# Tracing order kept on one engine instead of five, in a fused attention, Fourier mixing and feed-forward kernel

## The chip, the core and the metric

The kernel runs on one NeuronCore of a Trainium2 chip. The core has five instruction queues, each worked through strictly in the order in which its instructions stand: TensorE (PE, matrix products), VectorE (DVE), ScalarE (ACT), GpSimd (POOL) and SyncE (SP, which here only issues transfers). ACT and POOL can issue transfers too. The metric is the device time of one execution in microseconds (us); lower is better.

## The reference, cut to what matters

```python
# attention, per batch (8) and head (8): seq 576, head size 64
scores = q @ k.T / 8 ; cum = cumsum(max(s, 0))
scores = where(causal, -1e9, scores + minimum(-(cum_i - cum_j), 0))
attn = softmax(scores); x = attn @ v                 # -> (8, 576, 512)
# mixing and feed-forward
mixed = real(fft(fft(x, axis=seq), axis=model))
u = x + mixed
un = (u - mean(u)) / sqrt(var(u) + 1e-6)
out = u + relu(un @ w_ch1) @ w_ch2                   # 512 -> 2048 -> 512
```

## The kernel before

Everything is computed in pairs of numbers (a rounded high part and the rest, `h` and `l` in names), so most products are two or three matmuls.

**Attention.** 32 steps `i`, each one pair of heads of one batch. `load(i)` fetches q and k (`qk`); `high` casts them on ACT into the tile `KQ`; `low` makes the low parts, `k1` on DVE (L572) and `q1` on POOL (L575), out of copies that SP moves across partitions. `maxes(i)` computes each row's maximum: PE writes scores to PSUM (`pm`, L596), DVE reduces them (`Mx`, L603), PE transposes the ten columns (`pmt`) and SP writes them back into `KQ` (L613). `scores(i)` multiplies again (`ps`, L639 and L640), ACT takes the exponential (`P`, L643), POOL zeroes the upper triangle (L620, L624). `av(i)` multiplies by v (`pavA`, `pavB`, L672); ACT copies the result to `stage`. `post(i)` inverts the row sums: they travel by DMA into `sums` (L683), DVE adds and inverts (L693, L694), SP sends them through DRAM (`rd` L697, `rb` L701), POOL multiplies (L709), and SP spreads the result into `xs`.

**Mixing.** `folds` and `fourier`, once per batch, do the two transforms as matmuls with tables (`dcos`, `scos`, ...), which `load_tables` fetches through POOL's queue at step 2 of the main loop.

**Feed-forward.** `mlp()` goes over 9 token tiles of 512 and 16 slices of the hidden width. Layer 1 is 12 matmuls into `h` (L284), ACT and DVE split the result into `zh` (L289) and `zl` (L314), layer 2 is 12 matmuls into four `acc` banks (L340 to L342). Beside it run `mean`, `centre`, `deviation` and `output` of the neighbouring tiles, which load `uj` tiles over SP (L142), subtract the mean on DVE (L194) and write the result (`o`, L227 to L232).

**The weights' conversion.** The weights arrive as 64-bit floating point (`wP`). `convert(f, x, wc, buf)` turns one piece into a high and a low 32-bit part: a transfer in (L80), one DVE step (L84), one ACT step (L86), three DVE steps (L88, L89, L91), three POOL steps (L94, L96, L98) and a transfer out to `wD` in DRAM (L100). There are 20 pieces of 512 columns, in three buffers (two named `wide`, one `cv`), during main-loop steps 0 to 7, and 24 pieces of 256 columns, in two halves of `cv`, during steps 8 to 13. The feed-forward part starts once the first ten slices are converted, and fetches weights from `wD` through ACT's queue (`w`, L131).

**What sets the order.** All these are Python generators that yield a cost, and `weave` interleaves them: it always advances the stream that is behind by its share. The result is the order in which instructions are traced. The main loop runs under `tc.manual_schedule(engines={...})`: on the engines named there, instructions are issued in the order traced. On an engine that is not named, the framework's scheduler decides the order at build time: it walks through a modelled time and gives a free engine an instruction that is then ready by its model, the earliest traced first. In the kernel before, all five engines are named.

Of the kernel before, what the change touches and what calls it, by code (L numbers as in the profile page):

```python
# [8 lines left out]
F32 = mybir.dt.float32  # L9
F32R = mybir.dt.float32r  # L10
AF = mybir.ActivationFunctionType
ALU = mybir.AluOpType
BF16 = mybir.dt.bfloat16
I32 = mybir.dt.int32
# [26 lines left out]
def fused_kernel(ctx, tc, qkT, vA, sP, wP, tabD, tabS, corr, out):  # L41
    nc = tc.nc
# [11 lines left out]
    wD = dram.tile([NF, 128, 2, 2, 512], F32, name="wD")  # L54
# [8 lines left out]
    wbias = const.tile([128, 1], F32, name="wbias")  # L63
    nc.vector.memset(wbias, -8.0 * WEXP)

    def pool(name, **kw):
        return tc.tile_pool(name=name, bufs=1, reuse_waits="tile", **kw)


    mlp0 = ctx.enter_context(tc.tile_pool(name="mlp0", bufs=1))  # L70

# [4 lines left out]
    def convert(f, x, wc, buf):  # L76

        k, o = divmod(x * wc, 512)
        words, e = buf[:, 0:2 * wc], buf[:, 2 * wc:3 * wc]
        nc.sync.dma_start(out=words, in_=wP[f, :, wc * x:wc * x + wc].bitcast(I32))  # L80
        hi = words.rearrange("p (n w) -> p n w", w=2)[:, :, 1]
        lo = words.bitcast(U16).rearrange("p (n w) -> p n w", w=4)[:, :, 1]
        yield 2.0
        nc.vector.tensor_scalar(e, hi, 0x7FF00000, None, op0=ALU.bitwise_and)  # L84
        yield 1.0
        nc.scalar.activation(e, e, AF.Relu, bias=wbias, scale=8.0)  # L86
        yield 1.0
        nc.vector.scalar_tensor_tensor(out=e, in0=hi, scalar=-0x80000000, in1=e, op0=ALU.bitwise_and, op1=ALU.bitwise_or)  # L88
        nc.vector.tensor_scalar(hi, hi, 0xFFFFF, 0x100000, op0=ALU.bitwise_and, op1=ALU.bitwise_or)  # L89
        yield 0.5  # L90
        nc.vector.scalar_tensor_tensor(out=hi.bitcast(F32), in0=lo, scalar=2.0 ** -16, in1=hi, op0=ALU.mult, op1=ALU.add)  # L91
        yield 1.0
        v = e.bitcast(F32)
        nc.gpsimd.tensor_mul(v, hi.bitcast(F32), v)  # L94
        wh, wl = words[:, 0:wc], words[:, wc:2 * wc]
        nc.gpsimd.tensor_copy(wh.bitcast(F32R), v)  # L96
        yield 0.5
        nc.gpsimd.tensor_sub(wl.bitcast(F32R), v, wh.bitcast(F32))  # L98
        yield 1.5
        nc.sync.dma_start(out=wD[f, :, k, :, o:o + wc], in_=words.bitcast(F32).rearrange("p (s n) -> p s n", s=2))  # L100
        left[f] -= wc
        yield 1.5

    CONVERT = 9.0
    left = [1024] * NF
# [1 line left out]
    def convert_w(pieces, wc, places):  # L107

        def way(n):
            yield n * CONVERT / len(places)  # L110
            for f, x in pieces[n::len(places)]:
                yield from convert(f, x, wc, places[n]())
        yield from mixed(*[[way(n), 1.0] for n in range(len(places))])
# [617 lines left out]
    stages = mlp()  # L731

    order = ctx.enter_context(ExitStack())
    ET = mybir.EngineType
    order.enter_context(tc.manual_schedule(engines={ET.PE, ET.Activation, ET.DVE, ET.Pool, ET.SP}))
    for i in range(NP + 5):
        streams = []
        if 2 <= i <= NP + 1:
# [201 lines left out]
```

## Time and profile before

| what | value |
|---|---|
| median of 3 runs | 1648.24 us (1647.5 to 1652.3) |
| the profiled execution | 1643.94 us, of it 1642.2 us from the first instruction to the last |
| PE busy | 1386.4 us, 84% of the span |
| DVE, ACT, POOL busy | 700.8, 526.9, 491.6 us (43%, 32%, 30%) |
| mean granted TensorE clock | 0.921 |

The page of the profile gives busy time per engine, the span in 40 slices, DMA queues, the chain of work that ended last and groups of instructions. Other views used below: busy time in chosen stretches, the waits (who waited for whom), one tile's instructions, and the timeline. In a row of waits, "PE pm L596 <- DVE Mx L603: 26.1, 17, 4.7" means that PE's instruction at line 596 that writes `pm` stood idle 26.1 us in total, 17 times, 4.7 us at most, until DVE's line 603 was done. SPq is SP's queue issuing transfers.

### The profile page before, as it was taken

The numbers are of one execution on the slowest core, as the hardware profiler recorded it, in microseconds if no ns is written. First come the engines' busy times: TensorE is split into PE (matmuls) and PEld (weight loads), VectorE is DVE, ScalarE is ACT, GpSimd is POOL, SyncE is SP. The second block draws the span as 40 slices with busy tenths as digits, with TensorE's granted clock in tenths as the row PEclk, the third lists the DMA queues.
The fourth block names the chain that finished last, engine by engine and source line by source line (L and its number), as shares of the span: only waits on it lengthen the run. The fifth ranks groups of instructions, "written<-read, shape, count | busy, mean of one in ns | idle before, by whom it ended". The sixth has DMA issues, their size and how long they took to land.

```text
span 1642.2 us, 18338 instructions
## 1 busy us (share of the span) xinstructions
PE 1386.4 (84%) x6244; PEld 1116.2 (68%) x6244; DVE 700.8 (43%) x1567; ACT 526.9 (32%) x1149; POOL 491.6 (30%) x522
## 2 busy tenths in 40 slices
PE   4666665778877899889999889979897999999998
PEld 3444453556765687678777667757785887888887
DVE  5766745454445433543454334334423332222322
ACT  3443433433333423343344333334322221111210
POOL 4766654343433231233223212232212121020200
PEclk9877796889988999989999899989998999999999
DMA  5776554656655556645755564464456445320100
GB/s 160 198 209 199 168 175 156 183 173 183 213 170 179 164 183 171 210 123 184 223 174 171 178 188 153 140 205 145 142 164 218 164 157 166 129 77 26 54 25 26
DMA packets 118137, 259.84 MB, mean 158 GB/s; under 512 B 16047, under 2 KB 44112, under 8 KB 118043
## 3 DMA queue, kind: packets, MB, share of 16 engines
q1 hardware_dynamic: 87115, 150.25, 30.1%
q10 hardware_dynamic: 29232, 105.92, 20.4%
q0 software_dynamic: 1696, 2.50, 0.8%
q8 instruction: 50, 0.82, 0.2%
q14 instruction: 44, 0.36, 0.1%
HBM read 197.96 MB, written 36.70 MB: 143 GB/s over the span
## 4 chain that ended last, share of the span: by engine, by line
PE 52%; DMA 22%; DVE 8%; POOL 6%; issue 5%; ACT 3%; SPq 3%; ACTq 0%; POOLq 0%; DVEq 0%
PE h L284 19%; PE acc L340 6%; PE acc L342 6%; PE acc L341 6%; DMA uj<-uD 5%; PE pavB L672 5%; DMA w<-wD 3%; DMA cv<-in_wP_dram 3%; DMA wD<-cv 2%; PE pm L596 2%; PE ps L639 2%; PE ps L640 1%; DVE trash L603 1%; DMA uD<-xs 1%; DMA wD<-wide 1%
## 5 line engine op out<-in xcount | busy, mean ns | idle before, releaser
L314 DVE SCALAR_TENSOR_TENSOR zl<-h,zh 128x512 fp32r<-128x512 f32 x144 | 99.0, 688 | 354.9 <-ACT zh L289 354.4
L643 ACT ACTIVATE P<-ps 128x320 f32<-128x320 f32 (+4 forms) x384 | 146.6, 391 | 235.0 <-PE ps L640 230.8
L284 PE MATMUL h<-uch,w 128*128 128x512 f32 x688 | 189.7, 418 | 20.2 <-ACT uch L196 18.1
L596 PE MATMUL pm<-KQ 128*128 128x256 f32 (+3 forms) x384 | 144.0, 391 | 73.5 <-DVE Mx L603 35.5
L639 PE MATMUL ps<-KQ 128*128 128x256 f32 (+2 forms) x384 | 132.1, 346 | 78.0 <-DVE Mx L603 30.4
L603 DVE CUSTOM_DVE_ANT_0 trash<-pm,amask 128x128 bf16<-128x128 f32 (+3 forms) x256 | 123.8, 483 | 163.5 <-PE pm L596 157.5
L672 PE MATMUL pavB<-P,va 128*128 128x320 f32 (+2 forms) x640 | 170.4, 419 | 9.7 <-DVE Mx L603 7.2
L284 PEld LDWEIGHTS h<-uch,w 128*128 128x128 f32 x688 | 135.6, 202 | 54.2 <-ACT uch L196 24.2
L289 ACT ACTIVATE zh<-h 128x512 fp32r<-128x512 f32 x144 | 85.8, 596 | 261.0 <-PE h L284 260.5
L672 PEld LDWEIGHTS pavB<-P,va 128*128 128x128 f32 x640 | 129.9, 213 | 55.4 <-issue 15.2
L340 PE MATMUL acc<-zh,w 128*128 128x512 f32 x332 | 139.8, 421 | 27.9 <-DVE o L227 23.1
L596 PEld LDWEIGHTS pm<-KQ 128*128 128x128 f32 x384 | 79.1, 210 | 105.8 <-DVE Mx L603 48.9
L639 PEld LDWEIGHTS ps<-KQ 128*128 128x128 f32 x384 | 78.7, 205 | 101.0 <-DVE Mx L603 34.3
L620 POOL TENSOR_SCALAR_AFFINE_SELECT P<-P 128x512 f32<-128x512 f32 x64 | 49.9, 779 | 313.4 <-ACT P L643 312.9
L341 PE MATMUL acc<-zh,w 128*128 128x512 f32 x332 | 135.7, 409 | 0.0
L342 PE MATMUL acc<-zl,w 128*128 128x512 f32 x332 | 135.5, 408 | 0.0
L640 PE MATMUL ps<-q,k 128*128 128x256 f32 (+2 forms) x384 | 123.2, 323 | 0.0
L284 PE MATMUL h<-uch,W 128*128 128x512 f32 x464 | 117.4, 395 | 6.3 <-ACT uch L196 6.3
L284 PEld LDWEIGHTS h<-uch,W 128*128 128x128 f32 x464 | 88.0, 190 | 26.3 <-ACT uch L196 8.0
L204 POOL TENSOR_TENSOR t<-t,uj 128x512 f32<-128x512 f32 x27 | 36.1, 1339 | 225.3 <-ACT uj L202 224.3
L340 PE MATMUL acc<-zh,W 128*128 128x512 f32 x244 | 96.4, 395 | 8.3 <-DVE o L227 7.4
L575 POOL TENSOR_TENSOR q<-qk,q 64x576 fp32r<-64x576 f32 x64 | 94.5, 1478 | 20.4 <-DMA q<-KQ 15.5
(148 smaller groups left out, 2398.0 us busy)
## 6 DMA issues: line engine op xcount, KB each, us to landing
w<-wD ACTq DMA_DIRECT2D x169, 512.0 KB
uj<-uD SPq DMA_DIRECT2D x104, 256.0 KB
qk<-in_qkT_dram SPq DMA_DIRECT2D x32, 576.0 KB
W<-wD ACTq DMA_DIRECT2D x32, 512.0 KB
va<-in_vA_dram SPq DMA_DIRECT2D x32, 480.0 KB
q<-KQ SPq DMA_DIRECT2D x32, 288.0 KB
k<-KQ SPq DMA_DIRECT2D x32, 288.0 KB
rb<-rd SPq DMA_DIRECT2D x64, 144.0 KB
```

What stands on the lines that cost most here:

```text
L284: nc.tensor.matmul(h[:, :n], w[:, a, j * 128:(j + 1) * 128], b[:, j, :n], start=i == 0, stop=i == 11)
L314: nc.vector.scalar_tensor_tensor(out=zl[:, :n], in0=h[:, :n], scalar=0.0, in1=zh[:, :n].bitcast(F32), op0=ALU.max, op1=ALU.subtract)
L340: nc.tensor.matmul(acc[:, :n], b[:, 0, cs], y[:, :n], start=g == 0, stop=False)
L341: nc.tensor.matmul(acc[:, :n], b[:, 1, cs], y[:, :n], start=False, stop=False)
L342: nc.tensor.matmul(acc[:, :n], b[:, 0, cs], z[:, :n], start=False, stop=g == NF - 1)
L575: nc.gpsimd.tensor_sub(q1[64:128, h], qk[0:64, h], q1[0:64, h].bitcast(F32))
L596: nc.tensor.matmul(p[:, :n], qy[:, h, 128 * c:128 * c + 128], ky[:, h, k0:k0 + n], start=True, stop=True)
L603: nc.vector.tensor_tensor_reduce(out=trash[:nq, :n], in0=p[:nq, :n], in1=amask[:nq, m0:m0 + n], scale=1.0, scalar=first if x else NEG, op0 ...
L639: nc.tensor.matmul(p[:, :n], ky[:, h, ksl], qy[:, h, a:a + n], start=True, stop=False)
L640: nc.tensor.matmul(p[:, :n], k1[:, h, ksl], q1[:, h, a:a + n], start=False, stop=True)
L643: nc.scalar.activation(P[:, o:o + a + n - lo], p[:, lo - a:n], AF.Exp, scale=0.125)
L672: nc.tensor.matmul(p[:, a - lo:n], va[:, c, vs], P[:, o:o + w], start=c == 0, stop=c == cs[-1])
```

## The change

Three edits. `manual_schedule` names TensorE alone, so that DVE, ACT, POOL and SP get their order from the scheduler. Each step of the conversion is traced under `behind(engine)`, which lets the scheduler place it only behind the instruction that was traced last on that engine; nothing else has such a tie. The conversion's two transfers per piece are issued by POOL instead of SP, and the costs it yields between steps are spread a little differently (their sum stays 9.0).

```diff
+    ET = mybir.EngineType
+    def behind(engine):
+        return tc.issue_after(next(i for i in reversed(nc.cur_bb.bb.instructions) if i.engine == engine))
...
-        nc.sync.dma_start(out=words, in_=wP[f, :, wc * x:wc * x + wc].bitcast(I32))
+        with behind(ET.Pool):
+            nc.gpsimd.dma_start(out=words, in_=wP[f, :, wc * x:wc * x + wc].bitcast(I32))
...
-        yield 2.0
-        nc.vector.tensor_scalar(e, hi, 0x7FF00000, None, op0=ALU.bitwise_and)
+        yield 2.5
+        with behind(ET.DVE):
+            nc.vector.tensor_scalar(e, hi, 0x7FF00000, None, op0=ALU.bitwise_and)
...
-        nc.gpsimd.tensor_mul(v, hi.bitcast(F32), v)
+        with behind(ET.Pool):
+            nc.gpsimd.tensor_mul(v, hi.bitcast(F32), v)
...
-        yield 1.5
-        nc.sync.dma_start(out=wD[f, :, k, :, o:o + wc], in_=words.bitcast(F32).rearrange("p (s n) -> p s n", s=2))
+        yield 0.5
+        with behind(ET.Pool):
+            nc.gpsimd.dma_start(out=wD[f, :, k, :, o:o + wc], in_=words.bitcast(F32).rearrange("p (s n) -> p s n", s=2))
         left[f] -= wc
-        yield 1.5
+        yield 2.0
...
-    order.enter_context(tc.manual_schedule(engines={ET.PE, ET.Activation, ET.DVE, ET.Pool, ET.SP}))
+    order.enter_context(tc.manual_schedule(engines={ET.PE}))
```

Line numbers in the kernel after are 13 higher behind the conversion (L603 becomes L616, L693 L706, L575 L588); the conversion's own lines become L87 (in), L92, L95, L98, L99, L102, L106, L108, L110 and L113 (out). PE's instructions stand in the same order in both kernels. On the other four, what stands where has changed throughout. Counted over the two orders, DVE's inversions of the sums stand on average 15 places earlier among its 1569 instructions, its subtractions of the mean (L194, now L207) 28 places earlier, the maxima 7 places later and the conversion's steps 5 to 7 places later; ACT's casts into `KQ` stand 16 to 19 places earlier.

POOL, near the start of the program, before:

```order
L575 TENSOR_TENSOR q_159<-qk,q_159 64x576 x2
L575 TENSOR_TENSOR q_219<-qk,q_219 64x576 x2
L620 AFFINE_SELECT P<-P 128x4x128
L624 AFFINE_SELECT P<-P 128x64
L94 TENSOR_TENSOR wide<-wide 128x512
L96 CAST wide<-wide 128x512
L98 TENSOR_TENSOR wide<-wide 128x512
```

and now, from the last two of the nine table transfers on:

```order
L375 DMA ssin_89<-in_tabS_dram 96x870
L376 DMA cor<-in_corr_dram 97x258
L588 TENSOR_TENSOR q_219<-qk,q_219 64x576 x2
L87 DMA wide<-in_wP_dram 128x1024
L633 AFFINE_SELECT P<-P 128x4x128
L87 DMA wide<-in_wP_dram 128x1024
L637 AFFINE_SELECT P<-P 128x64
L633 AFFINE_SELECT P<-P 128x4x128
L637 AFFINE_SELECT P<-P 128x64
L106 TENSOR_TENSOR wide<-wide 128x512
```

The conversion's loads now stand between the zeroings of the triangle, and the nine table transfers (`dcos` to `cor`), which stood 22 rows further on, stand ahead of the second step's `q1`.

SP, in steps 2 and 3 of the main loop, before (L80 and L100 are the conversion's transfers):

```order
L697 DMA rd<-sums 32x36
L683 DMA sums<-stage 16x1x36
L80 DMA wide<-in_wP_dram 128x1024
L701 DMA rb<-rd 64x576 x2
L100 DMA wD<-cv 128x1024
L613 DMA KQ_118<-mt 1x10x128
L578 DMA va<-in_vA_dram 128x5x192
L683 DMA sums<-rows 16x1x36
L80 DMA cv<-in_wP_dram 128x1024
L538 DMA qk<-in_qkT_dram 128x1152
L567 DMA q_729<-KQ_119 64x2x576
```

and now:

```order
L710 DMA rd<-sums 32x36
L551 DMA qk<-in_qkT_dram 128x1152
L696 DMA sums<-stage 16x1x36
L714 DMA rb<-rd 64x576 x2
L591 DMA va<-in_vA_dram 128x5x192
L696 DMA sums<-rows 16x1x36
L580 DMA q_728<-KQ_119 64x2x576
L626 DMA KQ_118<-mt 1x10x128
```

The conversion's transfers are gone from this queue; the fetch of q and k (`qk`), which waits for POOL and DVE to have read the buffer's old content, now stands ahead of `rb`, and the maxima's way back into `KQ` stands behind the sums and the copy of the next step's `q1`.

DVE, about the middle of the program, before (step of `k_4761`):

```order
L572 TENSOR_TENSOR k_4761<-qk,KQ_118 64x576
L599 TENSOR_REDUCE M_4756<-pm 64x1
L603 ISA trash,Mx_127<-pm,amask,M_4756 64x320
L603 ISA Mx_127 64x1
L603 ISA trash,Mx_127<-pm,amask 128x128
L603 ISA Mx_127 128x1
L693 TENSOR_SCALAR sums<-sums 32x36
L694 RECIPROCAL sums<-sums 32x36
L603 ISA trash,Mx_127<-pm,amask 128x256
L603 ISA Mx_127 128x1
```

and the same step now:

```order
L184 TENSOR_TENSOR t<-t,uj 128x512
L185 TENSOR_TENSOR t<-t,uj 128x512
L706 TENSOR_SCALAR sums<-sums 32x36
L163 TENSOR_TENSOR tl<-t,th 128x512
L707 RECIPROCAL sums<-sums 32x36
L327 SCALAR_TENSOR_TENSOR zl<-h,zh 128x512
L207 TENSOR_TENSOR uj<-uj,mu 128x512
L585 TENSOR_TENSOR k_4761<-qk,KQ_118 64x576 x2
L207 TENSOR_TENSOR uj<-uj,mu 128x512
L616 ISA trash,Mx_127<-pm,amask 128x128
L616 ISA Mx_127 128x1
```

The inversion of the sums, the sums for the mean and the mean's subtractions stand ahead of all of this step's maxima, where the inversion stood in the midst of them before.

More of the change, by code (lines that the diff above doesn't have):

```diff
@@ L79, in convert @@
         words, e = buf[:, 0:2 * wc], buf[:, 2 * wc:3 * wc]
-        nc.sync.dma_start(out=words, in_=wP[f, :, wc * x:wc * x + wc].bitcast(I32))
+        with behind(ET.Pool):
+            nc.gpsimd.dma_start(out=words, in_=wP[f, :, wc * x:wc * x + wc].bitcast(I32))
         hi = words.rearrange("p (n w) -> p n w", w=2)[:, :, 1]
         lo = words.bitcast(U16).rearrange("p (n w) -> p n w", w=4)[:, :, 1]
-        yield 2.0
-        nc.vector.tensor_scalar(e, hi, 0x7FF00000, None, op0=ALU.bitwise_and)
+        yield 2.5
+        with behind(ET.DVE):
+            nc.vector.tensor_scalar(e, hi, 0x7FF00000, None, op0=ALU.bitwise_and)
         yield 1.0
-        nc.scalar.activation(e, e, AF.Relu, bias=wbias, scale=8.0)
+        with behind(ET.Activation):
+            nc.scalar.activation(e, e, AF.Relu, bias=wbias, scale=8.0)
         yield 1.0
-        nc.vector.scalar_tensor_tensor(out=e, in0=hi, scalar=-0x80000000, in1=e, op0=ALU.bitwise_and, op1=ALU.bitwise_or)
-        nc.vector.tensor_scalar(hi, hi, 0xFFFFF, 0x100000, op0=ALU.bitwise_and, op1=ALU.bitwise_or)
+        with behind(ET.DVE):
+            nc.vector.scalar_tensor_tensor(out=e, in0=hi, scalar=-0x80000000, in1=e, op0=ALU.bitwise_and, op1=ALU.bitwise_or)
+            nc.vector.tensor_scalar(hi, hi, 0xFFFFF, 0x100000, op0=ALU.bitwise_and, op1=ALU.bitwise_or)
         yield 0.5
-        nc.vector.scalar_tensor_tensor(out=hi.bitcast(F32), in0=lo, scalar=2.0 ** -16, in1=hi, op0=ALU.mult, op1=ALU.add)
+        with behind(ET.DVE):
+            nc.vector.scalar_tensor_tensor(out=hi.bitcast(F32), in0=lo, scalar=2.0 ** -16, in1=hi, op0=ALU.mult, op1=ALU.add)
         yield 1.0
         v = e.bitcast(F32)
-        nc.gpsimd.tensor_mul(v, hi.bitcast(F32), v)
+        with behind(ET.Pool):
+            nc.gpsimd.tensor_mul(v, hi.bitcast(F32), v)
         wh, wl = words[:, 0:wc], words[:, wc:2 * wc]
@@ L733, in fused_kernel @@
     order = ctx.enter_context(ExitStack())
-    ET = mybir.EngineType
-    order.enter_context(tc.manual_schedule(engines={ET.PE, ET.Activation, ET.DVE, ET.Pool, ET.SP}))
+    order.enter_context(tc.manual_schedule(engines={ET.PE}))
     for i in range(NP + 5):
```

## The prediction

> **What bounds the kernel now.** I read the busy time by stretches first, then who waits for whom in the stretches that have slack, then the rows of the steps that move.
>
> By stretches (PE busy, PEld, DVE, ACT, POOL with their counts, then granted clock, DMA share, GB/s):
>
> ```profile
> 60.00:320.00 260.00, 166.04 (x674) 126.65 (x674) 152.41 (x346) 106.18 (x241) 145.17 (x150) 0.79 0.62 182
> 320.00:520.00 200.00, 161.91 (x727) 128.74 (x725) 98.17 (x248) 70.20 (x163) 74.92 (x95) 0.89 0.62 190
> 520.00:760.00 240.00, 213.76 (x1019) 174.20 (x1019) 103.88 (x243) 89.69 (x199) 68.17 (x71) 0.94 0.55 169
> 760.00:1200.00 440.00, 393.10 (x1851) 319.70 (x1852) 179.71 (x435) 157.85 (x359) 115.71 (x119) 0.95 0.56 172
> 1200.00:1642.00 442.00, 419.62 (x1879) 344.41 (x1877) 126.33 (x198) 80.04 (x145) 55.20 (x49) 0.98 0.33 110
> ```
>
> From 1200 us on PE is busy 95% at a clock of 0.98: nothing to win there, little to lose. From 60 to 320 us PE is idle 94 of 260 us, and no other engine is full either (DVE 59%, POOL 56%): that stretch is bound by waits between queues. From 520 to 1200 us PE still idles 73 of 680 us. So order decides in the first 520 us, and somewhat up to 1200.
>
> Who makes PE wait, 60 to 320 us:
>
> ```profile
> PE pm L596 <- DVE Mx L603: 26.1, 17, 4.7
> PE ps L639 <- DVE Mx L603: 17.3, 2, 13.2
> PE pavB L672 <- DVE Mx L603: 7.0, 6, 2.7
> PE pavA L672 <- DVE Mx L603: 2.0, 2, 1.6
> ```
>
> That is 52.4 us of waiting for DVE's maxima, more than half of PE's idle time there. What holds DVE in the same stretch:
>
> ```profile
> DVE cv L84 <- DMA cv<-in_wP_dram: 28.6, 7, 6.4
> DVE wide L88 <- ACT wide L86: 20.4, 10, 4.7
> DVE cv L88 <- ACT cv L86: 15.4, 5, 5.4
> DVE wide L84 <- DMA wide<-in_wP_dram: 5.2, 5, 1.8
> ```
>
> All four are the conversion: 69.6 us in which DVE stands at a conversion step that is not ready, with maxima behind it. 52.4 against 69.6 gives the exchange rate that I use below: 0.75 us of PE for each us that the conversion holds a queue in this stage. It is an estimate, and an upper one, since some of the maxima were late for other reasons.
>
> **The change part by part.**
>
> *POOL issues 88 transfers more* (44 in, 44 out). Its only transfers so far are the nine tables:
>
> ```profile
> L359 POOL DMA_DIRECT2D dcos<-in_tabD_dram x2: 744/847/950, 66.9 to 69.7; - x2
> L361 POOL DMA_DIRECT2D scos<-in_tabS_dram x2: 571/574/576, 68.6 to 71.2; - x2
> 76.66 0.55 POOL L363 DMA_DIRECT2D cor<-in_corr_dram  x1 [4.35 <-DMA dcos<-in_tabD_dram]
> ```
>
> The 40 transfers of the large pieces and the 24 loads of small ones have one run of memory per partition, like scos and cor: 64 x 0.57 = 36.5 us. The 24 small stores have two, like dcos: 24 x 0.85 = 20.4 us. Together 57 us, in the stretch from 60 to 520 us, where POOL is busy 145.17 + 74.92 = 220 of 460 us. It rises to 277 us, 60%. I cost the issuing itself at nothing: POOL's idle 240 us cover it. Without that cover it would cost PE up to 57 x 0.75 = 43 us.
>
> *The loads' waits move from SP's queue to POOL's.* A piece may be loaded only when the store before it in its buffer has landed. SP waits for that now (all of the span):
>
> ```profile
> SPq L80 <- DMA wD<-cv: 53.5, 20, 7.2
> SPq L80 <- DMA wD<-wide: 50.0, 8, 8.8
> ```
>
> 103.5 us in 28 waits, 3.7 us each. On POOL the triangle's zeroings (PE's `pavA` and `pavB` need them), the `q1` subtractions (`ps` needs them) and the conversion's own steps queue behind such a wait, and a load that goes out later makes DVE's L84 (now L92) wait longer, with maxima behind. POOL is busy 48% of the time there, so 48% of the waiting falls on work: 50 us, and at 0.75 that is **+37 us**. From below: 0, if the scheduler puts each load where its store has landed. From above: all of it, 103.5 x 0.75 = 78.
>
> *SP is rid of 88 transfers and of those waits.* What PE suffers from SP's queue is short in the profile:
>
> ```profile
> PE ps L639 <- DMA KQ<-mt: 8.9, 4, 2.2
> ```
>
> I take half, **-4 us** (bounds -9 and 0; the maxima's way back now stands behind the sums, which eats part of it). The page "DMA: Bandwidth & Descriptors" of the Trainium skill, section "Issuing engines are not separate DMA queues", speaks against even that: transfers from any engine run on the same 16 DMA engines, and another issuer saves only the time to issue. By it this term is 0 and the sum 4 us higher; the 8.9 us row is too small to judge it.
>
> *DVE's conversion steps stand 5 to 7 places later, behind maxima that are ready.* This attacks the 52.4 us. All of it would be -52; nothing would be 0, if the loads come later by as much as the steps. I take half, **-26 us**.
>
> *Steps that hang on transfers run ahead.* The inversion of the sums stands 15 places earlier on DVE, ahead of maxima. It waits for a transfer out of the previous product. Pieces of the chain that ended last, with start and length:
>
> ```profile
> 111.36 2.42 DMA sums<-stage
> 165.49 3.82 DMA sums<-stage
> ```
>
> So 3.1 us each, and 32 such places. Now it hardly costs anything, because it stands late:
>
> ```profile
>   DVE sums L693: 5.0, 1
> ...
> SPq L697 <- DVE sums L694: 126.9, 16, 24.5
> ```
>
> DVE waited for sums once; SP, which sends the result on, waited for DVE 7.9 us a time. 15 places are 15 x 1642/1569 = 16 us of DVE's queue at its mean pace, twice the 7.9 us that were spare, so I expect DVE to meet an unlanded transfer there once per step. The ten steps before 520 us, at 0.75: 10 x 3.1 x 0.75 = 23. The 22 later ones in a stretch where DVE is 42% busy and PE has banks in reserve, at a third of that rate: 22 x 3.1 x 0.25 = 17. Together **+40 us**; bounds 0 and 32 x 3.1 x 0.75 = 74.
>
> *The subtractions of the mean stand 28 places earlier.* That should remove PE's wait for their result,
>
> ```profile
> PE h L284 <- ACT uch L196: 24.4, 11, 6.5
> ```
>
> of which I take three quarters, **-18 us** (bounds -24 and, since they too stand behind loads and ahead of maxima, +24). The longer wait for `o` stays, since those steps keep their places:
>
> ```profile
> PE acc L340 <- DVE o L227: 30.5, 15, 5.8
> ```
>
> *The tables go out at about 19 us instead of 67.* POOL's first table transfer, and the `q1` work between which they now stand:
>
> ```profile
> 66.93 0.95 POOL L359 DMA_DIRECT2D dcos<-in_tabD_dram  x1
> 15.85 2.77 POOL L575 TENSOR_TENSOR q<-qk,q 64x576 fp32r<-64x576 f32 x2 [5.04 <-DMA q<-KQ]
> 29.12 2.77 POOL L575 TENSOR_TENSOR q<-qk,q 64x576 fp32r<-64x576 f32 x2 [10.50 <-DMA q<-KQ]
> ```
>
> With `cor` above they take POOL from 66.93 to 77.21 us, 10.3 us, of it 4.35 us in which the ninth waits for the first to land. 18.6 + 10.3 = 28.9 us; the next `q1` starts at 29.1 now, so it just fits. The 2.5 MB also share the DMA engines with the first q, k and v. Bounds: -10 (the time at 67 us comes free) to +10; I take 0.
>
> The profiled execution took 1643.94 us, 1.7 us of it around this span:
>
> ```profile
> span 1642.2 us, 18338 instructions
> ```
>
> Sum: 0 + 37 - 4 - 26 + 40 - 18 + 0 = **+29 us**. Against the profiled execution that is 1673. The median of the runs is 1648.24, 4.3 us above that execution, so the forecast for the median is 1648 + 29 = **1677 us**, slower by 1.8%.
>
> **The rivals.**
>
> *Faster: the queues stop blocking each other.* In the traced order an engine stands at an instruction that is not ready while ready ones wait behind it; the scheduler picks ready ones. If its modelled time is close to the real one, the +37 and +40 vanish and the gains are whole: -52 - 24 - 9 = -85, or, at the values taken, -48: 1600 us, and with a third of the two losses left 1626. For it: the 69.6 us above are exactly such blocking, and no engine but PE is over 60% busy. Against it: the order is fixed at build, and real transfers vary (2.4 and 3.8 us in the two `sums` rows, waits of 3.7 us on average and up to 8.8 for `wD`), so a place that suits one landing is wrong for the next. It decides if DVE's waits at L92 and L706 stay below about 80 us in all. Middle of this case: 1612 us.
>
> *The same.* The losses come out at 60% (46 us) and meet the gains of 48. For it: POOL's and DVE's idle halves. Against it: it needs two sums of independent size to agree to 5 us. 1648 us.
>
> *Much slower: POOL becomes the bound of the first 520 us.* 220 us of work, 57 of issuing and 103.5 of waiting are 380 of 460 us with no overlap; each `q1` and each zeroing then comes late, and the conversion, which the feed-forward part waits for, stretches. Price: 78 for the waits in place of 37, 43 for the issuing in place of 0: 1677 + 41 + 43 = 1761 at the end, 1720 halfway. For it: POOL's own nine transfers already show 4.35 us lost to one landing. Against it: 80% is still not full.
>
> The conversion's first DVE step (shortest, median, longest in ns):
>
> ```profile
> L84 DVE TENSOR_SCALAR cv<-cv x30: 279/300/1483, 45.0 to 460.5; 128x256 int32<-128x256 int32 x24, 128x512 int32<-128x512 int32 x6
> ```
>
> The page "SBUF — State Buffer" of the Trainium skill, section "SBUF: two separate sides", would add to the much slower case: it says that GpSimd cannot write its transfers' descriptors while VectorE runs an instruction in a two-port mode. If each of the 88 waited once for a conversion step of 0.30 us, the median of L84, POOL would lose 26 us more, an estimate from that page and that row, and the sum would rise by 26 x 0.48 x 0.75 = 9 us; no row before shows such a wait.
>
> **How the numbers follow.** My forecast, slower by some 10 to 60 us, has 0.50; much slower 0.14; the same 0.10; faster 0.26. A difference of 0.3% (5 us) is about what a measurement of this kernel can tell from none. So faster 0.26, same 0.10, slower 0.64. The forecast's own range is 1655 to 1710. The range that holds 8 in 10 must take in half of the faster case and half of the much slower one, which leaves 0.13 and 0.07 out: 1612 to 1735.
>
> **What would show it.** The conversion's last store goes out at 464.7 us now:
>
> ```profile
> L100 SPq DMA_DIRECT2D wD<-cv x30: 320/379/1100, 57.2 to 464.7; - x30
> ```
>
> Right: POOL waiting for `wD` at L87 for 80 us or more; DVE waiting at L92 from 60 to 320 us longer than the 33.8 us (28.6 + 5.2) that it waits for loads at L84, and at L706 for `sums` some tens of us; PE's idle time from 60 to 520 us, 94 + 38 = 132 us, grown by 20 or more, with a lower granted clock there; the last store later than 464.7 us; `uch` gone from PE's waits; the stretch that begins at 1200 us now unchanged in length. Wrong: PE's waits for `Mx` halved in the first 320 us and the last store out no later than now, or a loss that sits behind 1200 us, where no term of mine lies.

## The result and the profile after

The kernel after takes 1562.23 us (median of 3 runs, 1559.16 to 1562.93) against 1648.24 us: a ratio of 0.947 (0.944 to 0.950). It is 86 us faster, where 29 us slower was forecast; the time lies below the range of 1612 to 1735 us. The profiled execution after has a span of 1560.2 us, that of before 1642.2 us. Disturbed runs are left out of the times and ratios below (of the four runs with the `uj` loads tied, two were). A profile shows one execution, and that one can lie several us off the median: 1643.9 against 1648 to 1652 us before, 1535.9 against 1528.8 us for the kernel with all four engines free. So a difference of a few us between parts of two profiles says little.

Since TensorE's order is the same in both kernels, the k-th matmul of one is the k-th of the other, and the span can be cut at the same points of the program. First before, then after, cut where before passes 60, 320, 522 and 1200 us (start:end and length in us, then busy us and instructions of PE, PEld, DVE, ACT, POOL, then granted clock, DMA share, GB/s):

```profile
60.00:320.00 260.00, 166.04 (x674) 126.65 (x674) 152.41 (x346) 106.18 (x241) 145.17 (x150) 0.79 0.62 182
320.00:522.00 202.00, 161.91 (x727) 128.74 (x725) 100.17 (x250) 70.33 (x163) 76.84 (x97) 0.89 0.62 191
522.00:1200.00 678.00, 606.87 (x2870) 493.90 (x2871) 281.58 (x675) 247.40 (x555) 181.96 (x187) 0.94 0.55 170
1200.00:1637.00 437.00, 419.62 (x1879) 344.41 (x1877) 124.16 (x195) 80.04 (x145) 55.20 (x49) 0.98 0.33 109
```

```profile
61.00:311.00 250.00, 162.03 (x674) 130.81 (x673) 169.92 (x353) 108.00 (x244) 174.22 (x196) 0.77 0.60 187
311.00:508.00 197.00, 157.53 (x727) 128.60 (x726) 103.12 (x257) 72.10 (x165) 101.04 (x131) 0.90 0.63 189
508.00:1122.00 614.00, 578.02 (x2872) 480.43 (x2871) 264.33 (x669) 247.15 (x551) 180.50 (x185) 0.98 0.64 190
1122.00:1555.00 433.00, 416.84 (x1879) 344.34 (x1878) 126.81 (x189) 79.59 (x144) 55.69 (x49) 0.99 0.32 106
```

The four parts shrink by 10, 5, 64 and 4 us, and the part ahead of them grows by 1. So 64 of the 82 us come from the third, the part in which attention and the feed-forward work run side by side and the conversion is over. In it PE's idle time falls from 71 to 36 us, and PE's busy time for the same matmuls from 607 to 578 us at a granted clock that rises from 0.94 to 0.98.

PE's longest waits over the whole span, before and after (one of 11.7 us for ACT's `KQ`, the same in both, is left out):

```profile
PE pm L596 <- DVE Mx L603: 35.5, 33, 4.7
PE acc L340 <- DVE o L227: 30.5, 15, 5.8
PE ps L639 <- DVE Mx L603: 30.4, 7, 13.2
PE h L284 <- ACT uch L196: 24.4, 11, 6.5
PE ps L639 <- ACT P L643: 23.5, 12, 5.4
PE ps L639 <- DMA KQ<-mt: 8.9, 4, 2.2
```

```profile
PE pm L609 <- DVE Mx L616: 39.9, 22, 5.6
PE ps L652 <- DMA KQ<-mt: 35.6, 9, 6.6
PE mu L167 <- ACT th L161: 11.8, 1, 11.8
PE pmt L621 <- DVE Mx L616: 10.8, 3, 6.0
PE acc L353 <- DVE o L240: 10.5, 6, 2.4
PE pavB L685 <- DVE Mx L616: 8.4, 5, 4.2
```

`uch` is gone from the list, `o` is down to a third, the scores' waits for maxima and `P` are down to 3.5 and 5.6 us, and one wait has grown most, for the maxima's way back over SP (`KQ<-mt`, 8.9 to 35.6 us). In the third part the waits for `o` and `uch` fall from 23.1 and 11.2 us to 1.6 and none. That is 33 us, nearly all of the 35 us by which PE's idle time falls there.

The new waits that the prediction feared, on DVE (61 to 311 us, then 508 to 1122 us) and on POOL (whole span):

```profile
DVE cv L92 <- DMA cv<-in_wP_dram: 26.1, 8, 7.0
DVE wide L92 <- DMA wide<-in_wP_dram: 20.0, 6, 9.5
```

```profile
DVE sums L706 <- DMA sums<-rows: 54.3, 15, 6.6
```

```profile
L87 POOL DMA_DIRECT2D cv<-in_wP_dram x30 | 17.0, 568 | 50.4 <-DMA wD<-cv 49.0 <-DVE cv L102 1.3
L87 POOL DMA_DIRECT2D wide<-in_wP_dram x14 | 8.0, 573 | 20.9 <-DVE Mx L616 13.2 <-DMA wD<-wide 7.7
L113 POOL DMA_DIRECT2D wD<-cv x30 | 21.8, 728 | 8.0 <-POOL cv L110 7.8 <-issue 0.2
L113 POOL DMA_DIRECT2D wD<-wide x14 | 8.2, 583 | 1.8 <-POOL wide L110 1.8
```

They exist: DVE waits for loads 46 us in the first stretch (34 before), and meets the sums' transfer 15 times at 3.6 us in the third. PE's waits for DVE's maxima in that third part (all rows with `Mx` or `M` together) are 16.0 us, 10.6 before, so little of DVE's 54.3 us reaches PE by that way.

### The profile page after: what moved, and what is told of

Read it like the earlier page. It is cut to its first block, busy times and chain, and to the rows that moved or that the text cites. A ratio compares the mean times of both kernels' runs of the same rounds, so it can differ in the third digit from the quotient of the medians.

```text
span 1560.2 us, 18514 instructions
## 1 busy us (share of the span) xinstructions
PE 1347.4 (86%) x6244; PEld 1107.7 (71%) x6244; DVE 705.9 (45%) x1567; ACT 529.8 (34%) x1149; POOL 548.1 (35%) x610
## 4 chain that ended last, share of the span: by engine, by line
PE 45%; DMA 13%; issue 9%; POOL 7%; DVE 6%; ACT 2%; SPq 1%; ACTq 0%; POOLq 0%; DVEq 0%
PE h L297 15%; PE acc L353 6%; PE acc L354 5%; PE acc L355 5%; PE pavB L685 5%; DMA uj<-uD 5%; DMA cv<-in_wP_dram 3%; PE ps L652 2%; PE ps L653 1%; PE pm L609 1%; DMA wD<-cv 1%; POOL o L242 1%; DMA w<-wD 1%; PE pyc L446 1%; DMA rb<-rd 1%
## 5 line engine op out<-in xcount | busy, mean ns | idle before, releaser
L609 PE MATMUL pm<-KQ 128*128 128x256 f32 (+3 forms) x384 | 142.5, 391 | 71.6 <-DVE Mx L616 39.9
L652 PE MATMUL ps<-KQ 128*128 128x256 f32 (+2 forms) x384 | 133.0, 348 | 64.3 <-DMA KQ<-mt 35.6
L616 DVE CUSTOM_DVE_ANT_0 trash<-pm,amask 128x128 bf16<-128x128 f32 (+3 forms) x256 | 124.4, 486 | 123.8 <-PE pm L609 117.6
L297 PE MATMUL h<-uch,w 128*128 128x512 f32 x688 | 174.6, 396 | 0.6 <-DVE Mx L616 0.6
L297 PEld LDWEIGHTS h<-uch,w 128*128 128x128 f32 x688 | 128.5, 191 | 26.5 <-DVE Mx L616 1.4
L353 PE MATMUL acc<-zh,w 128*128 128x512 f32 x332 | 136.0, 410 | 1.6 <-DVE o L240 1.6
L354 PE MATMUL acc<-zh,w 128*128 128x512 f32 x332 | 133.3, 402 | 0.0
L588 POOL TENSOR_TENSOR q<-qk,q 64x576 fp32r<-64x576 f32 x64 | 92.4, 1458 | 85.1 <-DMA q<-KQ 56.2
L633 POOL TENSOR_SCALAR_AFFINE_SELECT P<-P 128x512 f32<-128x512 f32 x64 | 46.3, 723 | 215.5 <-ACT P L656 205.4
L355 PE MATMUL acc<-zl,W 128*128 128x512 f32 x244 | 96.2, 394 | 6.0 <-DVE zl L327 6.0
```

The lines of the kernel that those rows point to most:

```text
L297: nc.tensor.matmul(h[:, :n], w[:, a, j * 128:(j + 1) * 128], b[:, j, :n], start=i == 0, stop=i == 11)
L353: nc.tensor.matmul(acc[:, :n], b[:, 0, cs], y[:, :n], start=g == 0, stop=False)
L354: nc.tensor.matmul(acc[:, :n], b[:, 1, cs], y[:, :n], start=False, stop=False)
L355: nc.tensor.matmul(acc[:, :n], b[:, 0, cs], z[:, :n], start=False, stop=g == NF - 1)
L588: nc.gpsimd.tensor_sub(q1[64:128, h], qk[0:64, h], q1[0:64, h].bitcast(F32))
L609: nc.tensor.matmul(p[:, :n], qy[:, h, 128 * c:128 * c + 128], ky[:, h, k0:k0 + n], start=True, stop=True)
```

## The experiments

The terms of the prediction's sum are numbered in its order: T1 POOL's issuing (0), T2 the loads' waits (+37), T3 the relief of SP (-4), T4 DVE's conversion steps (-26), T5 the inversions (+40), T6 the subtractions of the mean (-18), T7 the tables (0).

Two theories were set against each other. The prediction's: a few waits in named places set the time, and each can be priced alone. Its rival: in traced order every queue stands again and again at something that is not ready while ready work is behind it, and the free order gains on each engine by itself. All ratios are to the kernel before, on the same chip, with 95% intervals; the times of before in these runs are 1650 to 1652 us.

### One part at a time

**Only the transfers.** All five engines keep the traced order; the 88 transfers go to POOL, with the yields of the kernel after. The ties are dropped, as nothing is scheduled. The new yields move the conversion's steps on DVE and ACT by some 2 places on average; what that is worth is not separated from the transfers.

```diff
-            nc.sync.dma_start(out=words, in_=wP...)
+            nc.gpsimd.dma_start(out=words, in_=wP...)
-        nc.sync.dma_start(out=wD...)
+            nc.gpsimd.dma_start(out=wD...)
```

> All five engines keep the traced order, as before; only the conversion's two transfers per piece go to GpSimd's queue, with the costs yielded between steps of the kernel after. Theory A (the transfers are beside the point, the gain is all order): 1640 to 1656 us, and the loads' waits for wD just change queues. Theory B (the prediction's term: waits on GpSimd's queue reach TensorE at 0.75 us each): 1648 + 33 = 1681 us. Theory C (freeing SyncE of 88 transfers is what gained): 1600 us or less.

Measured: 1684.79 us, ratio 1.020 (1.0185 to 1.0216), a loss of 33 us. Matmul by matmul, nearly all of it comes early: the 988th on record stands at 390 us before and at 430 us here, 40 of the 42 us by which these two profiled executions differ. POOL's and DVE's waits from 56 to 347 us, the same stretch of the program, and then PE's:

```profile
POOL wide L87 <- DMA wD<-wide: 40.1, 8, 7.7
POOL cv L87 <- DMA wD<-cv: 24.1, 7, 6.7
```

```profile
DVE cv L92 <- DMA cv<-in_wP_dram: 47.5, 7, 12.1
DVE wide L92 <- DMA wide<-in_wP_dram: 7.4, 2, 5.5
```

```profile
PE pm L609 <- DVE Mx L616: 45.0, 17, 8.1
PE ps L652 <- DVE Mx L616: 20.7, 3, 13.3
PE ps L652 <- DMA KQ<-mt: 18.7, 6, 3.9
```

This is the chain that the prediction drew: POOL stands for `wD`, loads go out later, DVE stands at L92 for 55 us instead of 34, and the maxima behind it come late to PE (73.6 us of waiting for `Mx` in all rows, 52.4 before). It is not the whole: PE's wait for `KQ<-mt` grew by 10 us where T3 let it shrink. SP no longer stands for `wD`, but it stands longer at `rd`, which sends on the sums (45.7 us for maxima ahead of them on DVE, 5.0 before).

**One engine free.** One engine is left out of the traced order, the conversion's ties stay, and the transfers stay on SP. Only that engine's rows move.

```diff
-    order.enter_context(tc.manual_schedule(engines={ET.PE, ET.Activation, ET.DVE, ET.Pool, ET.SP}))
+    order.enter_context(tc.manual_schedule(engines={ET.PE, ET.Activation, ET.Pool, ET.SP}))   # DVE free
```

> Only VectorE is ordered by the scheduler; TensorE, ScalarE, GpSimd and SyncE keep the traced order, transfers stay on SyncE. Theory A1 (VectorE's queue held back o and the mean's subtractions between 520 and 1200 us): 1590 us or less, with TensorE's waits for o below 10 us. Theory A2 (the loads and casts that feed VectorE must come earlier too, so the engines must be freed together): 1625 to 1650 us.

> Only ScalarE is ordered by the scheduler. Theory A1 (VectorE's queue): 1640 to 1656 us, no change. Theory A2 (engines must be freed together): 1625 to 1650. Theory A3 (ScalarE's casts into KQ and its exponentials were the ones held back): 1600 us or less.

> Only SyncE, which issues transfers, is ordered by the scheduler; the conversion's transfers stay on it. Theory A1 (VectorE's queue): 1640 to 1656 us. Theory A2 (together): 1625 to 1650. Theory A4 (loads of uj, q, k and the sums' way were issued too late in the traced order): 1600 us or less.

> The kernel before with GpSimd's order alone left to the scheduler, transfers on SP. The other three engines alone gained 40, 27 and 46 us, 113 in all; the change gained 86 and pays up to 33 for its transfers, so that 119 are to be explained. If the gains add up, GpSimd's own is small: 1640 to 1651 us. If GpSimd's order matters by itself (its zeroings gate P): 1620 to 1635 us.

**All four free, transfers on SP.** The kernel after, but for the queue of the transfers and the yields, which are those of before.

```diff
-        with behind(ET.Pool):
-            nc.gpsimd.dma_start(out=words, in_=wP...)
+        with behind(ET.SP):
+            nc.sync.dma_start(out=words, in_=wP...)
```

> The kernel after with the conversion's transfers back on SP (its costs as before, its ties kept): four engines free, no change of queue. Theory A, the transfers cost what they cost alone whatever the rest does: 1562 - 33 = 1529 us. Theory B, scheduled queues place other work into the waits for wD, so the price on POOL is hidden: 1555 to 1565 us. Theory C, the transfers are worth something only where the queues are free (SP, free of conversion, serves the main loop): slower than after, 1570 to 1595 us.

Measured, with the length of each part of the program between the same matmuls, from the windows of the profiled executions:

| kernel | us | ratio (95%) | to 60 | 60 to 320 | 320 to 522 | 522 to 1200 | rest |
|---|---|---|---|---|---|---|---|
| before | 1648 to 1652 | 1 | 60 | 260 | 202 | 678 | 437 |
| transfers alone | 1684.79 | 1.020 (1.0185 to 1.0216) | 56 | 291 | 218 | 676 | 438 |
| DVE free | 1611.11 | 0.975 (0.973 to 0.977) | 55 | 261 | 196 | 654 | 442 |
| ACT free | 1623.80 | 0.984 (0.979 to 0.988) | 62 | 259 | 201 | 665 | 435 |
| SP free | 1605.40 | 0.972 (0.9705 to 0.974) | 58 | 259 | 195 | 654 | 430 |
| POOL free | 1637.46 | 0.992 (0.989 to 0.995) | 63 | 260 | 199 | 671 | 437 |
| all four free | 1528.84 | 0.926 (0.923 to 0.928) | 56 | 234 | 191 | 615 | 433 |
| after | 1562.23 | 0.947 (0.944 to 0.950) | 61 | 250 | 197 | 614 | 433 |

None of the four expectations for a single free engine was met: 1611, 1624, 1605 and 1637 us lie between the ranges that were set.

Three things follow. The engines' own gains are 2.5, 1.6, 2.8 and 0.8%, in all 7.8% before rounding; together they give 7.4%. The transfers cost 2.0% in traced order and 2.1% (0.947 less 0.926) in free order: theory A of the last expectation, 1529 us, was met, to the microsecond by luck (its four runs go from 1525 to 1536 us). And the price of the transfers lies ahead of 522 us, where the conversion is (5, 16 and 6 us in the last two rows), while the gain of the order lies mostly behind it.

The columns differ in kind. From 522 to 1200 us the engines add up: 24, 13, 24 and 7 us alone, 63 together. PE's waits for `o` and `uch` there fall from 34.3 us to 28.1 with DVE free, 28.7 with ACT, 17.6 with SP, 31.8 with POOL and none with all four, and its idle time by 13, 6, 17, 4 and 38 us. So the shorter idle time shows at PE mainly in these two waits. SP's queue held them up most, but none of the four alone.

From 60 to 320 us none of them gains anything alone, at most 1 us, and together they gain 26. PE's waits in that part with DVE free alone:

```profile
PE ps L652 <- ACT P L656: 43.3, 16, 13.0
PE mu L167 <- ACT th L161: 14.2, 1, 14.2
PE pm L609 <- ACT P L656: 7.9, 3, 4.0
PE pm L609 <- DVE Mx L616: 6.6, 8, 2.1
```

PE's waits for the maxima are down from 52.4 to 12.6 us, and it waits for the exponentials instead (9.8 us before at `ps`). With all four free the wait for the exponentials is 4.1 us and that for maxima 27.9 us, about half of what it was before; the longest is now the maxima's way back:

```profile
PE ps L652 <- DMA KQ<-mt: 22.6, 6, 7.0
PE pm L609 <- DVE Mx L616: 19.5, 18, 3.2
PE mu L167 <- ACT th L161: 8.1, 1, 8.1
```

### Leaving out one part of the change

**Without the ties.** `behind` does nothing, so that the scheduler may put the conversion's steps ahead of their traced place. (With the ties, two steps have none of their own: POOL's L108 and L110, which follow L106 by their data.)

```diff
-        return tc.issue_after(next(i for i in reversed(nc.cur_bb.bb.instructions) if i.engine == engine))
+        return ExitStack()
```

> The kernel after without the ties: the scheduler may place the conversion's steps anywhere, also ahead of what was traced before them. Theory A, the ties only keep the conversion from running early and matter little: 1555 to 1570 us. Theory B, without them the scheduler puts conversion steps ahead of the maxima that TensorE waits for, as these are ready early by its model: 1580 to 1650 us, with pm's wait for Mx well above 40 us.

Measured: 1582.27 us, ratio 0.959 (0.957 to 0.961), 20 us slower than after. The loss is ahead of 531 us, where the three first parts are 64, 264 and 203 us long (61, 250, 197 after). In the second part PE's wait for maxima at `pm` is 26.8 us against 18.5 after, and that for ACT's copies to `stage` 11.9 against 3.3. Over the whole span the wait at `pm` is 54.6 us against 39.9, above the 40 us that theory B set, and the time is at B's lower end. So the ties are worth a fifth to a quarter of the gain.

**SP kept in traced order,** transfers on POOL.

```diff
-    order.enter_context(tc.manual_schedule(engines={ET.PE}))
+    order.enter_context(tc.manual_schedule(engines={ET.PE, ET.SP}))
```

> The kernel after with SP kept in traced order (transfers on GpSimd's queue, so SP has none of the conversion's). Theory A, the gains of the engines add up: SP's 46 us are lost, 1605 us, all of it behind 500 us. Theory B, what SP's freedom gained alone was only getting past the conversion's waits for wD, which are gone from SP here: 1562 to 1572 us.

Measured: 1634.15 us, ratio 0.990 (0.987 to 0.994). Most of the gain is gone, 72 us, more than SP's 46 alone, and in all parts (271, 212, 635 and 447 us). Both theories missed. It seems that free DVE, ACT and POOL are paced by the one queue left in order; no run shows this further. Its longest waits (whole span):

```profile
SPq L626 <- ACT P L656: 289.5, 22, 22.4
SPq L245 <- POOL o L242: 146.9, 27, 37.6
SPq L626 <- ACT mt L624: 84.6, 7, 20.8
```

The second is 150.6 us in the kernel after, too. The first and the third, at the maxima's way back, are 35.6 and 12.6 us there, and 142.6 and 50.2 us in the kernel before.

### The steps of the prediction, moved by hand or tied

**The inversions earlier (T5), in the order of before.** Only DVE's two steps on the sums move, 10 places on average; every other row of all engines stays.

```diff
-        yield 3.0
+        yield 1.0
         nc.vector.tensor_scalar_add(sums, sums, 1e-9)
         nc.vector.reciprocal(sums, sums)
-        yield 0.5
+        yield 2.5
```

> The kernel before with one thing moved: DVE's two steps that add to and invert the sums stand 10 places earlier on average among its instructions (31 times), every other row of all five engines where it was. Theory A, the step of the prediction (T5: DVE waits for the sums' transfer, 40 us for 15 places): 1648 + 27 = 1675 us. Theory B, the late inversions hold up SP, whose 'rd' waits for them 116 us up to 1200 us with loads and results queued behind it, and the early ones let it go on: 1605 to 1635 us, the waits of PE for 'o' and 'uch' shorter. Theory C, both or neither: 1643 to 1653 us.

Measured: 1640.85 us, ratio 0.995 (0.992 to 0.997), a gain of 9 us. No theory's range was met; C misses by 2 us. DVE hardly met an unlanded transfer here, 6.6 us in 4 waits, so the run does not show what such waits cost PE. The large gain of theory B is not there either. SP's waits between 522 and 1200 us before, and in the same part here:

```profile
SPq L697 <- DVE sums L694: 101.8, 14, 16.7
SPq L613 <- ACT P L643: 82.2, 7, 13.9
SPq L613 <- ACT mt L611: 45.8, 6, 10.9
SPq L232 <- POOL o L229: 42.3, 12, 8.5
```

```profile
SPq L697 <- DVE sums L694: 25.4, 8, 6.1
SPq L613 <- ACT P L643: 99.2, 7, 20.8
SPq L613 <- ACT mt L611: 58.1, 6, 17.5
SPq L232 <- POOL o L229: 54.2, 12, 9.5
```

SP's wait for the sums fell by 76 us, and its three other longest waits grew by 41 us. PE's wait for `o` there stayed (23.1 and 23.5 us). The profiled execution is the slowest of the twelve, 1650.6 us, so where the 9 us were won can't be read from it.

**`zh` earlier on ACT, in the order of before.** With ACT free, `zh` stands 1.6 exponentials earlier; here it is traced so, and nothing else moves.

```diff
-            yield C1
             nc.scalar.activation(zh[:, :n], h[:, :n], AF.Relu)
+            yield C1
```

> The kernel before with ACT's zh traced 1.68 exponentials earlier on average (as far as the scheduler put it in the kernel after), every other row of all five engines in its place. Theory A, zh is what ACT gains by its free order (27 us): 1620 to 1632 us, the gain spread over 520 to 1200 us, and DVE's wait for zh (95 us) cut by a third or more. Theory B, many small waits, of which this is one: 1636 to 1648 us.

Measured: 1647.40 us, ratio 0.9987 (0.9966 to 1.0008), no difference. The waits that it aims at did shrink: ACT before the exponentials from 180.9 to 97.2 us, DVE before `zl` from 95.4 to 61.8 us. PE's waits for `o` and `uch` stayed (34.3 and 34.2 us in that part).

**Ties in the kernel after.** Each of these five keeps some steps from standing ahead of their traced place, by the same means as the conversion's; the last one is made on the kernel with all four engines free.

```diff
+        with behind(ET.DVE): nc.vector.tensor_sub(u[j][:, :n], u[j][:, :n], mu[:, :n])   # and t's sums, and o
```

> The kernel after with DVE's side steps of the feed-forward part (the sums and subtractions of the mean and the outputs' products 'o') tied like the conversion's, so that none stands ahead of its traced place. Theory A, T6 of the prediction: the uch wait comes back, 1562 + 18 = 1580 us. Theory B, these steps, with the clock that their gaps cost, are most of what was won between 520 and 1200 us: 1595 to 1625 us. Theory C, what frees 'o' and 'uch' is when their data come, not their place on DVE: 1556 to 1568 us.

```diff
+        with behind(ET.SP): nc.sync.dma_start(out=u[:, :n], in_=uD[j, :, t0:t0 + n])   # and out
```

> The kernel after with SP's side steps of the feed-forward part (the loads of uj and the results' way out) tied, so that none stands ahead of its traced place. Theory A, SP's own 46 us were these loads standing earlier: 1590 to 1610 us. Theory B, SP gained because nothing that waits long stands ahead of them any more, wherever they were traced: 1556 to 1570 us.

```diff
+            with behind(ET.Activation): nc.scalar.activation(zh[:, :n], h[:, :n], AF.Relu)
+                    with behind(ET.DVE): nc.vector.scalar_tensor_tensor(out=zl[:, :n], ...)
```

> The kernel after with ACT's zh and DVE's zl tied, so that they stand no earlier than traced (zh goes from 1.65 to 0.2 exponentials earlier). Theory A, ACT waiting at an exponential with a ready zh behind it was a main cost between 520 and 1200 us: 1585 to 1605 us, DVE's wait for zh from 42 us back towards 95 us. Theory B, many small waits, none of them large: 1560 to 1575 us.

```diff
+            with behind(ET.Activation): nc.scalar.copy(ky[64:128, h], qk[64:128, h])   # and qy
```

> The kernel after with ACT's casts into KQ tied, which stood 16 to 19 places earlier. Theory A, their early place is what ACT gains: 1580 to 1595 us. Theory B, many small waits: 1556 to 1572 us.

```diff
+        with behind(ET.SP): nc.sync.dma_start(out=va, in_=vA[st["b"], :, :, st["j"]])
```

> All four engines free, transfers on SP (1529 us), with the load of v (va) tied to its traced place on SP. In the kernel after SP stands 123 us before this load until TensorE has read the old tile, and TensorE waits 34 us for the maxima's way back (KQ<-mt) in the first 320 us. Theory A, the load blocks the way back: that wait mostly goes, 1505 to 1520 us. Theory B, the way back is late for its own reasons (mt's copy on ACT): 1524 to 1534 us.

| tied | us | ratio to before (95%) | against its base |
|---|---|---|---|
| mean and outputs on DVE | 1569.8 | 0.9515 (0.9475 to 0.9555) | +8 |
| `uj` loads and results on SP | 1574 | 0.955 (0.950 to 0.959) | +12 |
| `zh` and `zl` | 1586.3 | 0.962 (0.958 to 0.965) | +24 |
| casts into `KQ` | 1557.7 | 0.944 (0.9415 to 0.947) | -5 |
| `va`, all four free | 1525.9 | 0.9255 (0.923 to 0.928) | -3 |

Only the third row stands well clear of its base: the intervals of the first and the last two overlap those of their bases, and the second, from two runs, just leaves it. 1569.8 us misses C of its expectation by 2 us, 1574 us lies between A and B, and the `zh`, casts and `va` rows fall into A, B and B.

With the mean's steps tied, PE's wait for `uch` in the third part comes back to 2.8 us and that for `o` to 11.1 (1.6 after). Yet that part is as long as after (615 and 614 us) and its idle time no longer (32 and 36 us): PE's waits for maxima fell from 16.0 to 5.8 us instead. So T6's wait came back in part without its price. `zh` and `zl` matter in the free order (24 us, A's lower end) though `zh` alone was worth nothing in the traced one; DVE's wait for `zh` did not go back to 95 us as A expected (33.0 us), so its account of that loss is not shown. The casts' early place gains nothing. The `va` load is not what delays the maxima's way back: PE's wait for it stays at 21.4 us (22.6) from 56 to 290 us.

The fastest kernels are the last row and all four free on SP, which their intervals do not tell apart: 0.926 of before, 2% ahead of the kernel after.

## Why the prediction was wrong

**What held.** The sum of the transfers' terms. T1: POOL issues for 17.0 + 8.0 + 21.8 + 8.2 = 55.0 us, against 57 forecast; that this is hidden was not separated. T1 to T3 together were +33 us, and alone they cost 33 (1.020), in the free order 34. That it fits so closely is partly luck, since the parts were off. Alone, POOL waits 119.0 us for `wD`, and T3 had the wrong sign, as PE's wait for `KQ<-mt` grew by 10 us. In the kernel after POOL waits 56.7 us, not the 80 or more that were set as the mark, and the price shows mostly at `KQ<-mt` (34.0 us in the first part against 22.6 with the transfers on SP; for maxima 32.4 against 27.9). The page "DMA: Bandwidth & Descriptors" of the Trainium skill, section "Issuing engines are not separate DMA queues", says that issuing from several engines saves only the time to issue; here the issuer, with the new yields, was worth 33 us, as far as the waits above show through what stands behind the transfers in the issuing engine's queue. Whether a transfer lands later when POOL issues it was not measured. For the rule on two-port instructions (page "SBUF — State Buffer", section "SBUF: two separate sides") the rows show no such wait: an issue at L87 takes 568 to 573 ns, as the table's did before (574).

**What failed, by term.**

- T5, the inversions (+40, bounds 0 to 74). In the kernel after DVE waits for the sums 69.2 us in 18, not 99 us in 32. Ahead of 508 us, where 23 of the 40 us were set, it is 0.8 us in 2: the waits did not come. In the third part it is 54.3 us in 15 (68 in 22 were forecast), but PE's waits for maxima rose there by only 5.4 us, where 17 were set. What DVE's waits cost PE by other ways was not isolated. Moved by hand by two thirds of the way, the inversions met 4 unlanded transfers, not one per step, and gained 9 us, outside the bounds: in most steps 10 places were within what was spare.
- T4 and T6 (-26 and -18). With T5 they made -4 us for DVE. DVE's free order alone gave 40 us. In the first part the waits for maxima did go down, 52.4 to 32.4 us in the kernel after (18.5, 9.1, 4.2 and 0.6 at `pm`, `pmt`, `pavB` and `h`), near T4, and `uch` vanished as said. But "the longer wait for `o` stays, since those steps keep their places" put 30.5 us at nothing, and it fell to 10.5 us. The steps did keep their places, on average within one; so what was no longer late was something that they wait for. Freeing any one of the four queues shortens this wait in the third part (23.1 us before; 18.6, 15.1, 15.6 and 20.3 us with DVE, ACT, SP and POOL free).
- No term for the order on ACT, none on POOL but the tables, and for SP only the 8.9 us of `KQ<-mt`. Measured alone: 27, 14 and 46 us. This is the largest hole: 87 us of gain on three engines for which the sum held -4. I priced a queue by the waits that PE shows for it. SP's waits stand in its own rows, 101.8 us for the sums and 82.2 for `P` between 522 and 1200 us, and I read the first of them only as slack for DVE. What these queues held up stood in PE's own rows, too, as the waits for `o` and `uch`, 54.9 us, of which I took 18.
- No term for the clock. In the part from 522 to 1200 us, PE's busy time for the same work fell by 29 us, next to 35 us less idle time. Over the kernels run here the two go together (idle, busy, clock): 71, 607, 0.94 before; 65, 600, 0.95 with ACT free; 54, 600, 0.97 with SP free; 36, 578, 0.98 after. The same work at 0.98 instead of 0.94 takes 607 x 0.94 / 0.98 = 582 us, so the clock is most of the 29 us. That the gaps set the clock is likely from this, but no run isolates it, and the first part does not follow: idle 94 us at 0.79 before, 88 us at 0.77 after.

In sum: +33 for the transfers, as forecast; -119 for the order, where the terms made -4. The step that failed is that the order was priced at nearly nothing: T5's loss, the `o` wait that stays, and no term for ACT's, POOL's and SP's queues or for the clock. Of the 64 us won in the third part, where the terms made -1, 33 are PE's waits for `o` and `uch` and 29 its busy time at the higher clock. The rival "faster" had the right direction and, as far as the runs show, the right mechanism at the wrong size. Its -85 was made from three waits of PE, without `o`, and its middle of 1612 us lies between no loss left (1600) and a third of it (1626). The mark that I set for it was DVE's waits at L92 and L706 below 80 us in all. Over the whole span they are, in the kernel after:

```profile
DVE cv L92 <- DMA cv<-in_wP_dram: 72.2, 20, 7.0
DVE sums L706 <- DMA sums<-rows: 69.2, 18, 14.1
DVE wide L92 <- DMA wide<-in_wP_dram: 23.3, 8, 9.5
```

That is 165 us: the mark was missed and the case came true, so the mark did not tell the cases apart.

**The other marks.** Right: DVE's wait at L92 (46 against 34 us), L706 over the whole span, the last store (467.2 against 464.7 us), `uch`, the last part nearly unchanged (437 to 433). Wrong: PE's idle time in the first two parts did not grow by 20 us; for the same matmuls it fell from 134 to 127 us. Its clock went down in the first (0.79 to 0.77) and not in the second (0.89 to 0.90). T7 fits: the tables go out from 18.6 us on, and the part ahead of 60 us takes 61.

**What stays open.** Which steps carry the engines' gains. Of DVE's 40 us the inversions explain some 9, the mean's steps, by their tie, at most some 8, not clear of noise; of ACT's 27 us no single step is found in the traced order; of SP's 46 the `uj` loads and the results some 12, from two runs. Why the maxima's way back became PE's second longest wait is open, too. The hand-moved steps show a reason why no such list need exist: where one wait went, others grew, in the same queue (76 us off, 41 on), at another engine (`Mx` to `P`), or at PE itself (`o` and `uch` back, `Mx` off, the part as long). That this is all of it was not shown.

## What to carry to other kernels

A wait in an in-order queue costs what stands behind it, so moving a slow producer's transfers onto another engine's queue must be priced there: the 33 us here came from what stood behind them, though the forecast's parts fitted less well than its sum. The order of whole queues was not to be had wait by wait: one step moved by hand took 76 us of waiting off SP for 9 us of time, while leaving a whole queue to the scheduler gave 14 to 46 us, and four of them 122. A wait of PE on a step whose own place doesn't change (`o`) need not stay: it can hang on other queues. Where a kernel keeps all its engines in one traced order, try each engine free by itself first; and split a mixed change (here 2% lost in the transfers, 7.4% won in the order) before judging it.

## What the runs showed of the hardware

Between 522 and 1200 us, where TensorE is about 90% busy or more, its granted clock went with its gaps: 0.94 to 0.96 in the kernels with 67 to 71 us of gaps there, 0.98 in those with 32 to 36 us. From before to after, PE's busy time fell by 29 us beside 35 us of gaps. This is a correlation over the kernels run here; from 60 to 320 us it does not hold (88 us of gaps at 0.77, 94 at 0.79).
